# Low parts of the last even gates made by two transfers instead of a VectorE subtraction, with three-part even out-weights

## The chip, the cores and the metric

One core of a Trainium2 chip runs the whole program. The time is the device time of one execution in microseconds; the median of three runs is given. The profile is one more execution, with its own time.

## What is computed

```python
def _moe_ref(x, w_in, w_out):          # layer 1
    h = x @ w_in
    g = np.maximum(0.01 * h, h)
    return (g @ w_out).astype(np.float32)

def _moe2_ref(x, w_in, w_out):         # layer 2
    h = x @ w_in
    g = np.where(h > 0.0, h, np.exp(np.minimum(h, 0.0)) - 1.0)
    return (g @ w_out).astype(np.float32)
...
    f = lower_bound + (1.0 - lower_bound) * sigmoid(f_logit)
    h = f[:, t] * h + (1.0 - f[:, t]) * x[:, t]    # for t in range(6080), y[:, t] = h
...
    x = attn_out.reshape(6080, 256)    # then layer 1, then layer 2; w_in 256 x 2048, w_out 2048 x 256
```

A gated scan over 6080 rows of 256 values feeds two feed-forward layers. All data are 32-bit floats.

## The kernel before

**Tiles and stages.** The 6080 rows are cut into 12 chunks (eleven of 512 rows, the second of 448), counted here c0 to c11. Each layer's 2048 hidden columns are cut into four groups, q0 to q3. A step of the program is one (layer, chunk, group): the products of the chunk with the group's in-weights (`wI`), the activation, and the products of the gates with the group's out-weights, which add into the chunk's output banks. In a group the 128-column blocks with odd numbers and those with even numbers are kept apart: odd gates `aO` with weights `wO`, even gates `aE` with weights `wE`.

**Two parts for each operand.** TensorE multiplies in `float32r`. To keep more bits, every operand is split: the high part is a copy rounded to `float32r` (ScalarE, line 797 for gates), the low part is the value minus the high part (VectorE, line 801 for gates). A product is three matmuls, in `mm3` (lines 617 to 619): high by high, high weight by low gate, low weight by high gate. Gates lie in buffers of the pool `op`, 16 KB a partition, high part in the first half, low part in the second. There are seven of them.

**Fewer products.** The in-products of most steps, and the odd out-products of some, use a scheme of seven products where eight stand in the plain form (`seven` says where; lines 908 and 923 make the operands). The even gates always go the plain way, `straight("aE", "E", j)`.

**Order.** Nothing is issued while the kernel's Python runs through the steps. Each operation is given to `Plan` with a cost, a lateness (`late`), what it waits for, and what it takes from or gives back to a pool. `Plan.emit` then walks through a clock of its own and fixes the order of instructions on each engine. So the lateness written for an operation decides how many other matmuls are put ahead of those that need it.

**Around the change.** In layer 1 the even gates of a step are a Prelu (line 723) of `h`; in layer 2 they are made on VectorE in line 745 after a minimum (lines 738 or 740) and an exponential (line 743). Both rest on line 668, which adds the last in-product of the step. SP issues all transfers: the loads of x and f (line 560), layer 1's output to DRAM and back (989, 605), the weights of layer 2, which are split while layer 1 runs, put into DRAM (399, 401) and brought back over those of layer 1 between the layers (414), and the results (1002). GpSimd (POOL) does one operation on each weight as it is loaded (line 368) and otherwise nothing.

Of the kernel before, what the change touches and what calls it, by code (L numbers as in the profile page):

```python
# [9 lines left out]
F32 = mybir.dt.float32  # L10
# [102 lines left out]
def kernel(  # L113
# [54 lines left out]
    SEVEN = {1: (1, 2), 2: (0, 1)}  # L168

    def sums(l, u):  # L170

        return u[0] == "I" or u[0] == "O" and u[1] in SEVEN[l]

    def stored(u):
# [4 lines left out]
    size = {u: SO if u[0] == "E" or u[0] == "O" and not any(u[1] in v for v in SEVEN.values()) else SI for u in units}  # L179
    w = {u: const.tile([P, 2 * size[u]], F32R, name=f"w{u[0]}{u[1]}") for u in units}  # L180
    w2d = {u: dram.tile([P, 2 * stored(u)], F32, name=f"w2d{u[0]}{u[1]}") for u in units}
# [15 lines left out]
        "op": tiles(7, [P, 4 * CH], F32R, "op"),  # L197
# [22 lines left out]
    DMA, LATE, FAR, SGN = 0.475, 2.3, 4.5, 0.8  # L220

# [31 lines left out]
    def seven(l, c, q):  # L253

        return q in SEVEN[l] and not (l == 1 and c < 3) and not (l == 2 and c == NC - 1)

# [55 lines left out]
    def weights(l, u, due, gate=()):  # L312
# [41 lines left out]
        def lo():  # L354

            return w[u][:, size[u] : size[u] + m] if l == 1 else src()
# [29 lines left out]
        def src():  # L386
            return val()[:, :m]

        m = stored(u) if l == 2 else SO
        cp = act(s1(m), None, lambda: nc.scalar.copy(out=hi(), in_=src()), made,  # L390
                 take=[(b, "sp", "ws")] if l == 2 else [])
        sb = dve(v1(m), due, lambda: nc.vector.tensor_tensor(
            out=lo(), in0=src(), in1=hi().bitcast(F32), op=ALU.subtract,
        ), [cp], give=[(b, "wf", "ws")] if l == 1 else [])
        if l == 1:
            (wplain if aside else wdone)[l, u] = [sb]
            return
        was2.append(cp)
        a = dma(m / 586.0, None, lambda: nc.sync.dma_start(
            out=w2d[u][:, :m], in_=tile_("sp")[:, :m]), [cp], late=FAR)  # L400
        z = dma(m / 586.0, due, lambda: nc.sync.dma_start(
            out=w2d[u][:, m : 2 * m], in_=val()[:, :m]), [sb, a], give=[(b, "wf", "ws")], late=FAR)
# [3 lines left out]
    def reload(u, after):  # L406

        q = u[1] // 2 if u[0] == "I" else u[1]
        m = stored(u)

        def load(to, at, n):
            def run():
                dst, src = (t.rearrange("p (j m) -> p j m", j=2) for t in (w[u].bitcast(F32), w2d[u]))
# [5 lines left out]
        parts = [(0, 0, m // P)] if m < 8 * P else [(0, 7, 1), (1, 1, 6)]  # L419
        ready = wdone[2, u] + after  # L420
        wdone[2, u] = [dma(2 * part[2] * P / 590.0, due, load(*part), ready, late=LATE) for part in parts]

        def back(after):

            wdone[2, u] = [dma(0.5, due_in[-1 - NQ] - 3.0, load(0, 0, 1), after, late=LATE)]

        return back

    def wop(u, s):

        return tuple(w[u][:, j * size[u] + s * P : j * size[u] + (s + 1) * P] for j in (0, 1))
# [50 lines left out]
    def rows(c, filled, take, read=()):  # L482

        n = sizes[c]
        xb = {"rows": {}}
        bt = take

        def part(j, k):
            return xb["p"][2][:, 4 * HC * j + k * n : 4 * HC * j + (k + 1) * n]

        last = []
        for k in range(KD):
            def word(k=k):
                return bt["bt"][2][:, k * n : (k + 1) * n]
# [105 lines left out]
    def fetched(c, gates, hold):  # L600
        n = sizes[c]
        bt = {"pool": "bt"}
        filled = []
        for k in range(KD):
            filled.append(dma(DMA, None, lambda k=k: nc.sync.dma_start(
                out=bt["bt"][2][:, k * n : (k + 1) * n], in_=y1d[c][k * P : (k + 1) * P, :],
            ), gates + yd[c] + filled[:1], take=[(bt, "bt", "bt")] if k == 0 else [], late=LATE))
        ys[c] = operands(c, filled, bt, (), hold)


    def mm3(ps, wop, a, start, stop, whole=False):


        n = ps.shape[-1]
        parts = [slice(0, n)] if n < CH or whole else [slice(0, HC), slice(HC, CH)]
        for z, s in enumerate(parts):
            nc.tensor.matmul(ps[:, s], wop[0], a[0][:, s], start=start and z == 0, stop=False, skip_group_check=True)  # L617
            nc.tensor.matmul(ps[:, s], wop[0], a[1][:, s], start=False, stop=False, skip_group_check=True)  # L618
            nc.tensor.matmul(ps[:, s], wop[1], a[0][:, s], start=False, stop=stop, skip_group_check=True)  # L619
# [6 lines left out]
    def group(i):  # L626
# [10 lines left out]
        if l == 1 and c < 3:  # L637
            wo["O"] = wplain.get((l, ("O", q))) or wo["O"]
# [114 lines left out]
        def pieces():  # L753
# [5 lines left out]
            for r, s, bank, done, home in (("O", 1, "Y", C11, "seed"), ("E", 0, None, C22, None),  # L759
# [10 lines left out]
                else:  # L770
# [8 lines left out]
                hi = act(s1(2 * h), None, lambda a=a, g=g, s=s: nc.scalar.copy(out=view(a, 0, s), in_=half(g, s)),  # L779
# [3 lines left out]
                gates[r, s] = dve(v1(2 * h), None, lambda a=a, g=g, s=s: nc.vector.tensor_tensor(  # L783
                    out=view(a, 1, s), in0=half(g, s), in1=view(a, 0, s).bitcast(F32), op=ALU.subtract), [hi])
                kept.setdefault(r, [first_, hi])

# [7 lines left out]
        for name, g, done in (("aO", gO, odd), ("aE", gE, even)):  # L794
            if name == "aO" and apart or final:
                continue
            hi = act(s1(2 * n), None, lambda name=name, g=g: nc.scalar.copy(out=gate(name, 0), in_=whole(g)),  # L797
# [4 lines left out]
                out=gate(name, 1), in0=whole(g), in1=gate(name, 0).bitcast(F32), op=ALU.subtract,  # L802
# [24 lines left out]
        def turned(r, s, part):  # L827
# [7 lines left out]
            def wide(z, j):  # L835
                return w[r, q][:, z * size[r, q] + j * D : z * size[r, q] + (j + 1) * D]

            def run(fresh):
                for j in (0, 1):
                    for t in tiles_:  # L840
                        dst = yb[s][2][:, t % 2 * D : (t % 2 + 1) * D]
                        for z in (0, 1):
                            nc.tensor.matmul(dst, ops(part, j, t), wide(z, j), start=s in fresh and t % 2 + j + z == 0,  # L843
                                             stop=False, skip_group_check=True)
                            if part:
                                break
# [181 lines left out]
    for i, (l, c, q) in enumerate(stream):  # L1028
        back = [firsts[i - 6] if i >= 6 else None]
        if q == 0:  # L1030
            hold = firsts[i - 1 : i - 1 + 1] if i > 4 else []
# [13 lines left out]
        if l == 2 and c == NC - 1 and q in SEVEN[2]:  # L1045
            backs["O", q]([last_use[q][1]])
        at = len(prods)
        o = group(i)
        if l == 1 and c in (1, 2):
            for z in ([q - 1] if q else []) + ([q] if q == NQ - 1 else []):  # L1050
                for u in (("I", 2 * z), ("I", 2 * z + 1)) if c == 1 else (("O", z),):
                    if sums(1, u):
                        finish(u, [prods[-1], outs[-1]])
        firsts.append(prods[at])
        if l == 1 or c == NC - 2:
            last_use[q] = (prods[-1], o)
# [31 lines left out]
```

## Time and profile before

| | |
|---|---|
| median of the three runs | 994.54 us (994.28 to 1003.21) |
| profiled execution, its own time | 995.75 us |
| span of the profile | 993.9 us |
| TensorE matmuls busy | 982.4 us, 99% of the span, 8234 instructions |
| VectorE | 878.9 us, 88%, 1356 |
| ScalarE | 774.5 us, 78%, 1139 |
| GpSimd | 37.8 us, 4%, 38 |
| transfers on SP's queue | 73.08 MB, 27.4% of 16 DMA engines |

The profiled execution's time is 1.85 us longer than its span, and 1.2 us longer than the median. Busy times of matmuls overlap (each is 0.28 us long and the next starts 0.11 us later), so the distance from one start to the next is what a matmul costs. L with a number is a line of the kernel; `op<-ws,op` reads: writes a buffer of `op`, reads one of `ws` and one of `op`.

### The profile page before, as it was taken

What the parts mean: (1) busy time and instruction counts of PE and PEld (TensorE: products, weight loads), DVE (VectorE), ACT (ScalarE), POOL (GpSimd) and SP (SyncE); (2) the same over time, 40 slices, a digit from 0 to 9 for tenths busy, and PEclk for the clock granted to TensorE, in tenths of its full rate; (3) what the DMA queues carried; (4) which work ended last, traced back from release to release, by engine and by line L of the source; (5) the groups of instructions that cost most, each with busy time, mean ns of one, the idle gap of its engine ahead of it and who ended that gap; (6) DMA issues with size and microseconds to landing.
All of it is one profiled execution on the core that took longest, in us unless ns stands there. A gap on an engine that the chain in (4) does not pass through costs nothing.

```text
span 993.9 us, 20119 instructions
## 1 busy us (share of the span) xinstructions
PE 982.4 (99%) x8234; PEld 969.8 (98%) x8234; DVE 878.9 (88%) x1356; ACT 774.5 (78%) x1139; POOL 37.8 (4%) x38
## 2 busy tenths in 40 slices
PE   7999999999999999999999999999999999999998
PEld 6999999999999999999999999999999999999998
DVE  7899989999999999886678888988988989889875
ACT  6777787887878878867687878788877888788864
POOL 1122000100000010100000000000000000000000
PEclk9999999999999999999999999999999999999999
DMA  6542304435254443302760101101111021010110
GB/s 185 138 115 56 82 12 115 119 97 155 80 150 142 108 138 112 85 23 95 260 226 22 22 22 41 22 23 22 31 35 22 23 44 22 22 23 22 32 22 22
DMA packets 159853, 74.36 MB, mean 75 GB/s; under 512 B 133520, under 2 KB 147600, under 8 KB 159760
## 3 DMA queue, kind: packets, MB, share of 16 engines
q1 hardware_dynamic: 159760, 73.08, 27.4%
q8 instruction: 64, 1.05, 0.4%
q14 instruction: 29, 0.24, 0.1%
HBM read 48.01 MB, written 25.03 MB: 73 GB/s over the span
## 4 chain that ended last, share of the span: by engine, by line
PE 94%; DVE 4%; POOL 1%; issue 1%; DMA 0%; ACT 0%; DVEq 0%; SPq 0%
PE bank L617 28%; PE bank L618 28%; PE bank L619 28%; PE bank L843 2%; PE seed L619 2%; PE seed L618 2%; PE seed L617 2%; POOL ws L368 1%; DVE ws L378 0%; DVE op L801 0%; DVE ws L374 0%; DVE h L279 0%; DVE bt L585 0%; DMA raw<-in_f_logit_dram 0%; DVE up L365 0%
## 5 line engine op out<-in xcount | busy, mean ns | idle before, releaser
L617 PE MATMUL bank<-op,wI 128*128 128x256 f32 (+2 forms) x1136 | 318.1, 280 | 0.8 <-ACT sn L665 0.6
L618 PE MATMUL bank<-op,wI 128*128 128x256 f32 (+2 forms) x1136 | 317.3, 279 | 1.4 <-DVE op L498 1.4
L619 PE MATMUL bank<-op,wI 128*128 128x256 f32 (+2 forms) x1136 | 316.9, 279 | 0.0
L617 PEld LDWEIGHTS bank<-op,wI 128*128 128x128 f32 x1136 | 213.6, 188 | 3.7 <-ACT sn L665 0.9
L618 PEld LDWEIGHTS bank<-op,wI 128*128 128x128 f32 x1136 | 213.5, 188 | 3.6 <-DVE op L498 2.1
L619 PEld LDWEIGHTS bank<-op,wI 128*128 128x128 f32 x1136 | 213.5, 188 | 0.4
L618 PE MATMUL bank<-op,wE 128*128 128x256 f32 (+2 forms) x662 | 190.9, 288 | 0.0
L617 PE MATMUL bank<-op,wE 128*128 128x256 f32 (+2 forms) x662 | 190.8, 288 | 0.0
L619 PE MATMUL bank<-op,wE 128*128 128x256 f32 (+2 forms) x662 | 190.7, 288 | 0.0
L618 PE MATMUL bank<-op,wO 128*128 128x256 f32 (+2 forms) x672 | 187.7, 279 | 0.0
L617 PE MATMUL bank<-op,wO 128*128 128x256 f32 (+2 forms) x672 | 187.7, 279 | 0.0
L619 PE MATMUL bank<-op,wO 128*128 128x256 f32 (+2 forms) x672 | 187.6, 279 | 0.0
L668 DVE TENSOR_TENSOR h<-bank,sn 128x512 f32<-128x512 f32 (+1 forms) x176 | 120.1, 682 | 36.3 <-PE bank L619 30.0
L617 PEld LDWEIGHTS bank<-op,wO 128*128 128x128 f32 x672 | 126.3, 188 | 0.4
L619 PEld LDWEIGHTS bank<-op,wE 128*128 128x128 f32 x662 | 124.3, 188 | 2.3
L619 PEld LDWEIGHTS bank<-op,wO 128*128 128x128 f32 x672 | 126.2, 188 | 0.3
L618 PEld LDWEIGHTS bank<-op,wO 128*128 128x128 f32 x672 | 126.2, 188 | 0.3
L665 ACT COPY sn<-bank 128x512 f32<-128x512 f32 (+1 forms) x176 | 102.6, 583 | 30.0 <-PE bank L619 28.3
L617 PEld LDWEIGHTS bank<-op,wE 128*128 128x128 f32 x662 | 124.5, 188 | 1.3
L618 PEld LDWEIGHTS bank<-op,wE 128*128 128x128 f32 x662 | 124.3, 188 | 1.2
L801 DVE TENSOR_TENSOR op<-h,op 128x1024 fp32r<-128x1024 f32 (+1 forms) x78 | 95.6, 1226 | 8.9 <-ACT op L797 8.4
L801 DVE TENSOR_TENSOR op<-ws,op 128x1024 fp32r<-128x1024 f32 (+1 forms) x72 | 86.1, 1209 | 15.1 <-ACT op L797 15.1
(112 smaller groups left out, 1770.5 us busy)
## 6 DMA issues: line engine op xcount, KB each, us to landing
ws<-in_moe_w_in_dram SPq DMA_DIRECT2D x32, 255.6 KB, 3.7
ws<-in_moe_w_out_dram SPq DMA_DIRECT2D x32, 255.6 KB, 3.3
w2dI<-ws SPq DMA_DIRECT2D x16, 448.0 KB, 3.0
wI<-w2dI SPq DMA_DIRECT2D x8, 896.0 KB, 5.8
y1d<-t SPq DMA_DIRECT2D x22, 256.0 KB, 2.0
bt<-y1d SPq DMA_DIRECT2D x22, 256.0 KB, 2.8
raw<-in_f_logit_dram SPq DMA_DIRECT2D x80, 64.0 KB, 3.0
raw<-in_x_dram SPq DMA_DIRECT2D x80, 64.0 KB, 2.5
```

The lines of the kernel that those rows point to most:

```text
L368: sg = pool(SGN, None, lambda: nc.gpsimd.tensor_scalar(out=fr(), in0=top().bitcast(I8), scalar1=2.0, scalar2=-2.0, op0=ALU.min, op1=ALU.ma ...
L617: nc.tensor.matmul(ps[:, s], wop[0], a[0][:, s], start=start and z == 0, stop=False, skip_group_check=True)
L618: nc.tensor.matmul(ps[:, s], wop[0], a[1][:, s], start=False, stop=False, skip_group_check=True)
L619: nc.tensor.matmul(ps[:, s], wop[1], a[0][:, s], start=False, stop=stop, skip_group_check=True)
L665: return act(s1(2 * h), None, lambda: nc.scalar.copy(out=ps(name), in_=ps("X")), after, take=[(b, name, "sn")])
L668: return dve(v1(2 * h), None, lambda: nc.vector.tensor_tensor(out=half(name, s), in0=two(ps(bank)), in1=two(ps(sn)), op=ALU.add), after, **k)
L801: gates[name] = dve(v1(2 * n), None, lambda name=name, g=g: nc.vector.tensor_tensor(out=gate(name, 1), in0=whole(g), in1=gate(name, 0).bit ...
L843: nc.tensor.matmul(dst, ops(part, j, t), wide(z, j), start=s in fresh and t % 2 + j + z == 0, stop=False, skip_group_check=True)
```

## The change

Three things are edited, and the set of products stays as it is (the table `SEVEN` is written in another form with the same members; `back`, `finish` and the names `parts`, `cut`, `pieces` follow from that).

1. For q3 of both layers (`LOWS`), except the very last step, the even gates' low part is no longer a VectorE subtraction. A transfer on SP copies the gates into the low half of the `op` buffer, ScalarE writes minus the high part into the high half, and a transfer issued by GpSimd adds the high half onto the low half (`late_low`). The planner is told 0.475 + 3.0 us for the copy and 1.3 + 5.0 us for the addition.
2. For this the high part of all even gates is stored negated, so the even weights are kept in three parts: high, minus high, and minus low. `mm3` and `turned` take the second for the product with the gates' high part. The weight tiles `wE` grow from 2 to 3 parts, ScalarE makes the new one, and layer 2's `wE` goes to DRAM and back with it.
3. The pool `op` has six buffers in place of seven.

```diff
-    w = {u: const.tile([P, 2 * size[u]], F32R, name=f"w{u[0]}{u[1]}") for u in units}
-    w2d = {u: dram.tile([P, 2 * stored(u)], F32, name=f"w2d{u[0]}{u[1]}") for u in units}
+    def parts(u):
+        return 3 if u[0] == "E" else 2
+    w = {u: const.tile([P, parts(u) * size[u]], F32R, name=f"w{u[0]}{u[1]}") for u in units}
+    w2d = {u: dram.tile([P, parts(u) * stored(u)], F32, name=f"w2d{u[0]}{u[1]}") for u in units}
...
-        "op": tiles(7, [P, 4 * CH], F32R, "op"),
+        "op": tiles(6, [P, 4 * CH], F32R, "op"),
...
+    LOWS = ((1, NQ - 1), (2, NQ - 1))
+    SWD, CCE, COPY = 1.3, 5.0, 3.0
...
+        ends = [sb]
+        if minus:
+            turned = w[u][:, m : 2 * m] if l == 1 else None
+            ends.append(act(s1(m), due, lambda: nc.scalar.mul(
+                out=turned if l == 1 else tile_("sp").bitcast(F32R)[:, m : 2 * m], in_=hi().bitcast(F32), mul=-1.0), [cp]))
...
+        three = ((0, 0), (0, 1), (1, 0)) if len(wop) == 2 else ((1, 0), (0, 1), (2, 0))
...
+            for t, (g, v) in enumerate(three):
+                nc.tensor.matmul(ps[:, s], wop[g], a[v][:, s], start=start and z == t == 0, stop=stop and t == 2,
+                                 skip_group_check=True)
...
+        def late_low(g, done):
+
+            def low():
+                return gate("aE", 1).bitcast(F32)
+
+            got = plan.add("-", 0.0, None, lambda: None, done, take=[(b, "aE", "op")])
+            cp = dma(DMA, None, lambda: nc.sync.dma_start(out=low(), in_=whole(g)), [got], late=COPY)
+            hi = act(s1(2 * n), None, lambda: nc.scalar.mul(out=gate("aE", 0), in_=whole(g), mul=-1.0),
+                     [got, *highs[-1:]])
+            free([cp, hi], [(b, g, home)])
+            ad = pool(SWD, None, lambda: nc.gpsimd.dma_start(
+                out=low(), in_=gate("aE", 0).bitcast(F32), accum_op=ALU.add), [hi, cp], late=CCE)
+            highs.append(hi)
+            for s in (0, 1):
+                tops["E", s], gates["E", s] = hi, ad
+            gates["aE"] = ad
...
+            if name == "aE" and (l, q) in LOWS:
+                late_low(g, done)
+                continue
```

In layer 2, TensorE's order ahead of the even products of q3 of chunk c4, before (lines 617 to 619 are the three matmuls of `mm3`; `wO3`, `wE3` are q3's out-weights, `wI2` and `wI3` in-weights of the next chunk's q0):

```order
L619 MATMUL bank1_116<-op0_122,wO3_77 128x256
L617 MATMUL bank4_119<-op4_126,wI2_65 128x256
L618 MATMUL bank4_119<-op4_126,wI2_65 128x256
L619 MATMUL bank4_119<-op4_126,wI2_65 128x256
L617 MATMUL bank4_119<-op4_126,wI3_66 128x256
L618 MATMUL bank4_119<-op4_126,wI3_66 128x256
L619 MATMUL bank4_119<-op4_126,wI3_66 128x256
L617 MATMUL bank2_117<-op3_125,wE3_78 128x256
```

The same place of the changed kernel (the three matmuls now share line 632; DMASW is the semaphore of a transfer issued by GpSimd):

```order
L632 MATMUL bank3_118<-op0_122,wO3_77 128x256 x6
L632 MATMUL bank6_121<-op4_126,wI2_65 128x256 x3
L632 MATMUL bank6_121<-op4_126,wI3_66 128x256 x3
L632 MATMUL bank2_117<-op4_126,wI2_65 128x256 [waits Activation_49]
...
L632 MATMUL seed0_114<-op1_123,wI3_66 128x256 x3
L632 MATMUL bank2_117<-op4_126,wI2_65 128x256 [waits Activation_49]
L632 MATMUL bank2_117<-op4_126,wI2_65 128x256 x2
L632 MATMUL bank2_117<-op4_126,wI3_66 128x256 x3
L632 MATMUL bank4_119<-op3_125,wE3_78 128x256
L632 MATMUL bank4_119<-op3_125,wE3_78 128x256 [waits DMASW2_49]
```

Three more pairs of in-products now stand between the odd and the even products: from the last in-matmul of the step itself to the first even one there are 115 matmuls before and 127 after, and the second even one is the first that waits for the added low part.

VectorE's order around q3's even gates of layer 2, before (line 745 makes the gates, the second line 801 their low part):

```order
L668 TENSOR_TENSOR h0_130<-bank5_120,sn2_139 128x2x256 [waits PE_49]
L740 TENSOR_SCALAR ws2_136<-h0_130 128x1024 [waits DVE_49]
...
L745 SCALAR_TENSOR_TENSOR ws2_136<-ws2_136,h0_130 128x1024 [waits Activation_49]
L971 TENSOR_TENSOR h1_131<-h1_131 128x256
L801 TENSOR_TENSOR op4_126<-ws0_134,op4_126 128x1024 [waits Activation_49]
L801 TENSOR_TENSOR op0_122<-ws2_136,op0_122 128x1024 [waits Activation_49]
```

The same place of the changed kernel (lines 682, 754, 759 and 838 are the former 668, 740, 745 and 801):

```order
L682 TENSOR_TENSOR h2_131<-bank2_117,sn2_138 128x2x256 [waits PE_49]
L748 SCALAR_TENSOR_TENSOR ws1_134<-ws1_134,seed0_114 128x2x256 [waits Activation_49]
L754 TENSOR_SCALAR ws2_135<-h2_131 128x1024 [waits DVE_49]
L748 SCALAR_TENSOR_TENSOR ws1_134<-ws1_134,bank3_118 128x2x256
L1017 TENSOR_TENSOR raw2_141<-h0_129 128x512
L759 SCALAR_TENSOR_TENSOR ws2_135<-ws2_135,h2_131 128x1024 [waits Activation_49]
L838 TENSOR_TENSOR op4_126<-ws1_134,op4_126 128x1024 [waits Activation_49]
```

The even gates' subtraction is gone from VectorE; the odd gates' one stays, and 23 instructions of 1358 leave the engine in all.

SP's order around the same gates in the changed kernel (line 618 loads the next chunk's input, line 1043 stores results; the copy of line 809 is new):

```order
L618 DMA bt0_128<-y1d5_100 128x512 [waits DMAHW4_49,DVE_49]
L618 DMA bt0_128<-y1d5_100 128x512 [waits DMAHW5_49]
L809 DMA op4_126<-ws1_134 128x1024 [waits DMAHW6_49,DVE_49,PE_49]
L1043 DMA out_0_dram<-t1_143 32x16x32 [waits DMAHW7_49,DVE_49]
...
L1043 DMA out_0_dram<-t0_142 32x16x32 [waits DMAHW2_49,DVE_49]
```

The copy stands between the loads and the stores, so SP comes to the stores behind it only when the gates are done. On GpSimd the additions alternate in layer 1 with the operations on weights (line 375, the former 368); in layer 2 they stand alone. 23 copies and 23 additions are new, 12 in layer 1 and 11 in layer 2.

## Rows read from the trace of the kernel before

**Rows 1.** Waits of TensorE: who waited for whom, total us, times, longest us.

```profile
PE bank L547 <- DMA raw<-in_f_logit_dram: 1.7, 2, 0.9
...
PE bank L618 <- DVE op L498: 1.4, 3, 0.6
PE bank L617 <- ACT sn L665: 0.6, 1, 0.6
PE seed L619 <- DVE wI L392: 0.3, 1, 0.3
```

**Rows 2.** Windows of 20 us, busy us (instructions) by engine, TensorE's granted clock, DMA share.

```profile
20.00:40.00 20.00, 19.01 (x127) 17.42 (x126) 18.20 (x26) 15.11 (x27) 4.23 (x5) 1.00 0.45 126
...
820.00:840.00 20.00, 20.00 (x177) 20.00 (x176) 19.26 (x31) 15.79 (x23) 0.00 (x0) 1.00 0.03 4
```

**Rows 3.** Groups by shape, TensorE's weight loads for the even products.

```profile
L617 PEld LDWEIGHTS bank<-op,wE 128*128 128x128 f32 x662 | 124.5, 188 | 1.3
...
L618 PEld LDWEIGHTS bank<-op,wE 128*128 128x128 f32 x662 | 124.3, 188 | 1.2
```

**Rows 4.** Groups by shape, the gates' split (busy us, mean ns) and the minimum of line 740.

```profile
L801 DVE TENSOR_TENSOR op<-h,op 128x1024 fp32r<-128x1024 f32 x70 | 86.7, 1239 | 7.2 <-ACT op L797 6.8
L801 DVE TENSOR_TENSOR op<-ws,op 128x1024 fp32r<-128x1024 f32 x66 | 79.5, 1220 | 14.7 <-ACT op L797 14.7
...
L797 ACT CAST op<-ws 128x1024 fp32r<-128x1024 f32 x66 | 68.1, 1050 | 2.9 <-DVE ws L734 1.4 <-DVE ws L745 1.3
...
L740 DVE TENSOR_SCALAR ws<-h 128x1024 f32<-128x1024 f32 x23 | 15.9, 690 | 0.4
```

**Rows 5.** Timeline of ScalarE near the start: start us, us, what.

```profile
26.98 0.57 ACT L496 CAST op<-bt 128x448 fp32r<-128x448 f32 x1 [0.30 <-DVE bt L585]
```

**Rows 6.** Timeline of VectorE near the start, the low part that follows.

```profile
28.21 0.61 DVE L498 TENSOR_TENSOR op<-bt,op 128x448 fp32r<-128x448 f32 x1
```

**Rows 7.** Timeline of TensorE, layer 2, q3: last in-matmul and first even matmul.

```profile
776.57 0.28 PE L619 MATMUL bank<-op,wI 128*128 128x256 f32 x1
...
789.60 0.28 PE L617 MATMUL bank<-op,wE 128*128 128x256 f32 x1
```

**Rows 8.** Timeline of VectorE, the even gates of the same step.

```profile
779.92 1.22 DVE L745 SCALAR_TENSOR_TENSOR ws<-ws,h 128x1024 f32<-128x1024 f32 x1
```

**Rows 9.** Timeline of SP, 770 to 782 us.

```profile
776.07 0.82 SPq L605 DMA_DIRECT2D bt<-y1d  x2
```

**Rows 10.** Timeline of TensorE, layer 1, q3: last in-matmul and first even matmul.

```profile
254.91 0.28 PE L619 MATMUL bank<-op,wI 128*128 128x256 f32 x1
...
267.26 0.28 PE L617 MATMUL bank<-op,wE 128*128 128x256 f32 x1
```

**Rows 11.** Timeline of ScalarE, the even gates of that step.

```profile
256.38 1.06 ACT L723 ACTIVATE h<-h 128x1024 f32<-128x1024 f32 x1
```

**Rows 12.** DMA issues: count, KB each, median us from issue to landing.

```profile
w2dO<-ws SPq DMA_DIRECT2D x4, 512.0 KB, 3.5
...
wE<-w2dE SPq DMA_DIRECT2D x4, 512.0 KB, 4.5
wO<-w2dO SPq DMA_DIRECT2D x2, 768.0 KB, 5.3
...
wI<-w2dI SPq DMA_DIRECT2D x8, 896.0 KB, 5.8
```

**Rows 13.** GpSimd's operations on tile ws: duration ns min/median/max, first and last start.

```profile
L368 POOL TENSOR_SCALAR ws<-ws x32: 636/812/4309, 7.9 to 397.7; 128x512 f32<-128x512 int8 x32
```

**Rows 14.** Line 399's stores of 256 to 512 KB during layer 1.

```profile
DMA to landing us min/median/max: 2.0/2.7/4.4
```

**Rows 15.** Windows of the stretches after q3's even gates (columns as in rows 2).

```profile
257.70:267.70 10.00, 10.00 (x90) 10.00 (x90) 9.90 (x15) 9.93 (x17) 0.87 (x1) 1.00 0.60 172
...
499.70:509.70 10.00, 10.00 (x91) 10.00 (x90) 5.93 (x10) 7.24 (x11) 0.00 (x0) 1.00 0.73 286
...
781.40:791.10 9.70, 9.70 (x88) 9.70 (x88) 8.97 (x18) 7.13 (x10) 0.00 (x0) 1.00 0.01 3
```

More of the change, by code (lines that the diff above doesn't have):

```diff
@@ L167 @@
     SI, SO = 7 * P, 2 * D
-    SEVEN = {1: (1, 2), 2: (0, 1)}
+    SEVEN = {(1, 1): range(3, 12), (1, 2): range(3, 12), (2, 0): range(0, 11), (2, 1): range(0, 11)}
     def sums(l, u):
-        return u[0] == "I" or u[0] == "O" and u[1] in SEVEN[l]
+        return u[0] == "I" or u[0] == "O" and len(SEVEN.get((l, u[1]), ())) > 0
     def stored(u):
@@ L253, in seven @@
     def seven(l, c, q):
-        return q in SEVEN[l] and not (l == 1 and c < 3) and not (l == 2 and c == NC - 1)
+        return c in SEVEN.get((l, q), ())
     due_in = [0.0]
@@ L354, in lo @@
         def lo():
-            return w[u][:, size[u] : size[u] + m] if l == 1 else src()
+            at = (parts(u) - 1) * size[u]
+            return w[u][:, at : at + m] if l == 1 else src()
         def val():
@@ L418, in reload, with back @@
         due = due_in[first[2, "w", q]] + (-12.0 if u[0] == "I" else 0.0)
-        parts = [(0, 0, m // P)] if m < 8 * P else [(0, 7, 1), (1, 1, 6)]
+        pieces = [(0, 0, m // P)] if m < 8 * P else [(0, 7, 1), (1, 1, 6)]
         ready = wdone[2, u] + after
-        wdone[2, u] = [dma(2 * part[2] * P / 590.0, due, load(*part), ready, late=LATE) for part in parts]
-        def back(after):
-            wdone[2, u] = [dma(0.5, due_in[-1 - NQ] - 3.0, load(0, 0, 1), after, late=LATE)]
+        wdone[2, u] = [dma(parts(u) * piece[2] * P / 590.0, due, load(*piece), ready, late=LATE) for piece in pieces]
+        def back(i, after):
+            wdone[2, u] = [dma(0.5, due_in[i] - 3.0, load(0, 0, 1), after, late=LATE)]
         return back
     def wop(u, s):
-        return tuple(w[u][:, j * size[u] + s * P : j * size[u] + (s + 1) * P] for j in (0, 1))
+        return tuple(w[u][:, j * size[u] + s * P : j * size[u] + (s + 1) * P] for j in range(parts(u)))
     S4, A11, A22, A12, S1, S2, S3 = range(7)
@@ L835, in wide @@
             def wide(z, j):
-                return w[r, q][:, z * size[r, q] + j * D : z * size[r, q] + (j + 1) * D]
+                at = z * size[r, q] + j * D
+                return w[r, q][:, at : at + D]
+            three = ((0, 0), (0, 1), (1, 0)) if r == "O" else ((0, 1), (0, 2), (1, 0))
             def run(fresh):
@@ L841, in run @@
                         dst = yb[s][2][:, t % 2 * D : (t % 2 + 1) * D]
[L842 to L846, printed above, removed]
+                        for y, z in three:
+                            if y == part:
+                                nc.tensor.matmul(dst, ops(part, j, t), wide(z, j),
+                                                 start=s in fresh and t % 2 + j + part == 0 and z == three[0][1],
+                                                 stop=False, skip_group_check=True)
             out_((2 - part) * len(tiles_), run, (s,), [(gates if part else tops)[r, s], *wo[r]])
@@ L1030 @@
         if q == 0:
[L1031 removed]
+            hold = firsts[-1:] if i > 4 else []
             if l == 1:
```

55 lines of the change are left out of this document (28 added, 27 removed).

## The prediction

> **What bounds the kernel now.** I read the waits of TensorE first, since a kernel whose matmuls are 99% busy can only gain what TensorE still waits. The view names 7 waits with some 7 us in all, and over half of that lies in the first five microseconds, before there is data [rows 1]. What is left is one wait of three times for VectorE's line 498 near the start and three single ones, some 2.5 us in all. Then the windows: from 40 us on each 20 us stretch holds nearly 20 us of matmul at a granted clock of 1.00, which is 2.4 GHz, while VectorE stands at 19.26 of 20 in layer 2 [rows 2]. The reader is to see that a busy VectorE delays nobody here. The third thing to read is the distance between two starts: from the last in-matmul of a step to its first even matmul 13.03 us pass for 115 matmuls, 0.1133 us each [rows 7]. The changed kernel issues the same 8224 matmuls of the same widths, so TensorE's stream keeps its length, and the change can only alter the waits in it.
>
> **What is removed.** 23 subtractions leave VectorE, 11 of full width in layer 1 and 10 in layer 2 at 1.24 and 1.22 us, and two narrower ones: 28 us of busy time [rows 4]. On the path lies only what TensorE waited for VectorE, 1.7 us of it, most of it at the start where no subtraction has left yet. I take a gain of 0.5 us, with 0 and 2.5 us (all the waits that are left) as ends.
>
> **What is added at no cost.** ScalarE makes the negated part of `wE` eight times, some 0.6 us each (the time of its 512-column casts, [rows 5] shows 0.57 for 448 columns), and multiplies by -1 where it copied; it has a fifth of its time free [rows 2]. The one place near the path is the first: the new operation stands ahead of the cast of line 496, which ran from 26.98 to 27.55 [rows 5]. It would end some 0.3 us later, and VectorE takes up the low part only at 28.21 [rows 6], so it stays covered; uncovered it would cost 0.6 us once. The even products change their order of weights, and no two neighbours share a weight any more. The trace shows that this was worth nothing: the second of two equal loads takes 188 ns like the first [rows 3]. The layer-2 `wE` is stored with 256 KB more and comes back as 768 KB, 5.3 us in place of 4.5 [rows 12]: 3.2 us more of transfers in a stage whose DMA engines are 73% busy [rows 15]. No wait of TensorE for a weight's return stands in the view of waits, so I take 0, with 3.2 us as the other end.
>
> **The new path, and its room.** In the 23 steps the low part now comes from copy, GpSimd's issue and addition, one after the other. The room for it is read from the trace and the order. In layer 2 the last in-matmul starts at 776.57 [rows 7] and the gates are done at 779.92 + 1.22 = 781.14 [rows 8], 4.57 us later. In the changed order the first matmul that waits is the 128th after it: 128 x 0.1133 = 14.50 us. The room is 14.50 - 4.57 = 9.93 us, and that order stands for nine of the eleven steps of layer 2; the two beside the narrow chunk have 0.2 and 0.6 us less. VectorE's order between the last in-product and line 745 (now 759) holds one operation more, line 1017, but the minimum comes one operation earlier, so I leave the 4.57 us as they are. In layer 1 the gates are done at 256.38 + 1.06 = 257.44 [rows 11], 2.53 us after the last in-matmul [rows 10]; the order has 115 matmuls there in five steps, 121 in two, 109 in two and 127 in one, which leaves 10.6, 11.3, 9.9 and 12.0 us. The first two chunks have 10.7 us or more by the same count.
>
> The trace of before has no copy inside SBUF and no adding transfer. For the copy of 512 KB the nearest rows are a store of 512 KB, 3.5 us, and a load of 512 KB, 4.5 us [rows 12]; I take 3.5, since it reads the same memory and the stage of the 4.5 was crowded. For GpSimd's issue the nearest row is its operation on weights, 0.64 to 4.31 us with a median of 0.81 [rows 13]; I take 0.85. For the addition the ends are 3.5 (as a plain 512 KB) and 6.6 us, where 896 KB take 5.8 and a line through 512 and 896 KB gives 6.6 for twice 512 KB [rows 12]; I take 4.7, near the middle. The sum is 3.5 + 0.85 + 4.7 = 9.05 us, under the room of 9.93 by 0.9, so layer 2 costs nothing. The ends are 3.5 + 0.64 + 3.5 = 7.6 and 4.5 + 0.85 + 6.6 = 12.0 us, the latter 2.0 us late in each step.
>
> The addition reads two streams of 512 KB where a copy reads one; the trace of before can't show what that costs. The Trainium skill says in "Collectives: The Full Stack", section "The bandwidth ceiling: the fold count and why AG ≠ RS ≠ AR", that an adding transfer is slow not for its arithmetic but because it needs two source reads on the same read ring, and halves the rate. That speaks against this change: by it the addition would be nearer to the 6.6 us, the sum 10.95 us, and each step of layer 2 late by 1.0 us.
>
> **Queues.** On SP the copy waits for the gates. Ahead of it stand the next chunk's two input loads, which were issued at 776.07, five microseconds before the gates [rows 9], and behind it only stores of results, whose buffers VectorE's transposes need again a chunk later. In layer 1 loads of x and f and of weights stand behind it, which wait for buffers of their own. GpSimd's additions alternate in layer 1 with its weight operations; it is idle nearly all the time, and a weight operation delayed by an addition feeds a layer that is hundreds of microseconds away.
>
> **Other traffic.** In layer 2 the DMA engines are free in that stretch, 1% [rows 15]. In layer 1 they are 18 to 60% busy there, the fullest at 257.7 [rows 15], and stores that take 2.7 us in the middle took up to 4.4 there [rows 14]. With 1.7 us more the 9.05 would become 10.75, a little late against 10.6 and 0.8 us late against 9.9. I count 1.5 us for some five full steps together, with 0 and 12 us as ends (1.7 us for copy and addition both, in six steps, less the 1.5 us spare). Layer 1's last addition meets the return of the layer-2 weights [rows 15]: I take 0.6 us once, with 0 and 4 as ends.
>
> **The sum.** -0.5 + 0 + 0 + 1.5 + 0.6 = +1.6 us on the profiled execution's 995.75, which gives 997.35, and on the median, 1.2 us lower, 994.54 + 1.6 = 996.1 us.
>
> **Rivals.**
> *The path is longer than its room (slower).* The point from which it decides is 9.9 us for copy, issue and addition. At 10.95 us layer 2 loses 1.0 x 11, layer 1 0.35 x 5 + 1.05 x 2, some 15 us: 1010 us. At 12.0 it is 2.1 x 11 + 1.4 x 5 + 0.7 x 2 + 2.1 x 2 = 36 us: 1031 us. For it speaks the addition's double reading, against it that DMA is nearly idle in layer 2 and that 9.05 rests on rows of the same size. Chance 0.18.
> *GpSimd's issue is stretched by VectorE (slower).* Its operation on weights took up to 4.31 us while VectorE was full [rows 13, 2]. Were each issue 3 us longer, the sum would be 12 us and the time again 1031. It would need this in most steps, while the median of the 32 is 0.81. Chance 0.05. The Trainium skill, "SBUF — State Buffer", section "Who interferes with whom", narrows this: only VectorE's two-port forms hold up the writing of descriptors. The row that shows such a form is line 740, 690 ns for 1024 columns where line 801 takes 1220 [rows 4]; by that rule an issue is delayed by at most 0.7 us, which the 0.9 us of room still hold.
> *Six `op` buffers are too few.* In the changed order 54 of ScalarE's 304 writes into `op` wait for TensorE, 19 before. If each of the 35 new waits made an operand 0.3 us late (the small waits of TensorE are 0.3 to 0.6 us, [rows 1]), it would be +10 us: 1005 to 1007 us. Against it: the releasing matmul stands well ahead of the reader of the buffer in TensorE's own order. Chance 0.07, half of it over 1%.
> *VectorE's relief pays (faster).* The bound is the 2.5 us of waits, 992.0 us; more than 1% would need TensorE's stream to be shorter. Chance of over 1%: 0.02.
>
> **How the numbers follow.** A measurement of this kernel tells about 1%, 10 us, from no change. The forecast, hidden but for a few steps (-2.5 to +10 us), has 0.68. Faster is 0.02. Of the rivals' 0.30 that are slow, 0.07 stay within 1%. So same is 0.75 and slower 0.23. The range begins at 992.0, where all waits are gone, and ends at 1012, past the nearer price of the first rival; above it lie the second's 0.05 and half of the first's, some 0.15, below it 0.02.
>
> **What would show it.** Matmul counts and VectorE less by 28 us show the removal. The waits of TensorE should hold no line with more than some 3 us for GpSimd's transfer, above all none in layer 2; the DMA issues should show the copy near 3.5 us and the addition near 4.7. A wait of q3's even matmuls of 1 us or more in each chunk is the first rival; long issues on POOL are the second; waits for other `op` writers on ScalarE and VectorE the third. The forecast is wrong if the addition is slower than 5.6 us.

## The result, and the profile after

The changed kernel took 1004.77 us (median of 13 runs, 999.82 to 1006.87) against 995.46 us (13 runs, 994.28 to 1003.78) for the kernel before. The ratio on record is 1.0065, 95% interval 1.0042 to 1.0088; it is not that of the two medians, which is 1.0094. That is slower, by less than the 1% that the prediction called the bound, and inside its range; the forecast of 996.1 us was 8.7 us too low. The runs of each kernel here fall into bunches several us apart, by slow spacings of matmuls that the experiments show, so a median also tells in which bunch most runs were. The profiled execution of the changed kernel took 1004.97 us.

First the page: busy us, share of the span and instructions of each engine.

```profile
PE 988.8 (99%) x8234; PEld 973.3 (97%) x8234; DVE 858.7 (86%) x1333; ACT 780.7 (78%) x1147; POOL 55.9 (6%) x61
```

TensorE has the same 8234 matmuls, VectorE 23 instructions less. The two full-width groups of VectorE's split, which answer to [rows 4], have lost 25.2 us (141.0 in place of 166.2), with the mean of one as before. All durations of VectorE add up to 26.7 us less; its busy time on the page fell by 20.2 us, since there overlaps count once. The groups now:

```profile
L838 DVE TENSOR_TENSOR op<-h,op 128x1024 fp32r<-128x1024 f32 x59 | 72.6, 1230 | 10.6 <-ACT op L833 10.4
L838 DVE TENSOR_TENSOR op<-ws,op 128x1024 fp32r<-128x1024 f32 x56 | 68.4, 1222 | 12.1 <-ACT op L833 11.2
```

The new path stands in the DMA issues (count, KB each, median us to landing) and in the queues (packets, MB, share of 16 engines); these answer to [rows 12]:

```profile
q0 software_dynamic: 3312, 11.93, 6.3%
...
op<-op POOLq DMA_DIRECT2D x21, 512.0 KB, 4.7
...
op<-h SPq DMA_DIRECT2D x11, 512.0 KB, 3.2
...
op<-ws SPq DMA_DIRECT2D x10, 512.0 KB, 2.9
```

Both count from the start of the issue. The addition's 4.7 us thus hold GpSimd's issue too, where the sum had 0.85 + 4.7; the copy takes 2.9 to 3.2 in place of 3.5. But a median hides a tail. The same additions, asked for by the tile that they write (GpSimd's issue in ns min/median/max; who waited, us, times; landing min/median/max):

```profile
L813 POOL DMA_DIRECT2D op<-op x23: 859/862/1021, 89.8 to 956.2; - x23
...
  PEld bank L632: 3.9, 5
  PE bank L632: 2.7, 3
...
DMA to landing us min/median/max: 4.2/4.7/10.1
```

By this view five steps of 23 waited, and one addition took 10.1 us. The waits of TensorE, which answer to [rows 1], name three of them and a snapshot (line 679) that cost 0.6 us before:

```profile
PE bank L632 <- DMA op<-op: 2.7, 3, 1.3
...
PE bank L632 <- ACT sn L679: 0.9, 2, 0.5
PE bank L632 <- DVE op L511: 0.8, 2, 0.6
```

These lines explain less than 3 of the 10.2 us by which the last matmul starts later in the new trace. (The span is 9.3 us longer: from the last start to the end 3.9 us pass in place of 4.8.) For the rest I took the start of every matmul in each trace and sorted the distance to the next. A spacing that is over 25 ns above the usual (113.3 ns at 256 columns, 226 at 512, 198 at 448, 100 at 224, 57 at 128) is a gap, and what is above the usual is its length. The other spacings at 256 columns are nearly all of two kinds: 112 to 115 ns, and 116 to 120 ns, at a granted clock of 1.00 both; from 116 ns on the excess over 113.3 is summed apart, as slow spacings. All kernels of this study, in us:

```
               gaps by stretch of the span            slow spacings  last
               0-40  40-200  200-560  560-end   all   number    us   start    rest
before         13.6     1.5      0.8      0.4  16.2      739   3.5   989.1   969.4
after          14.6     0.8      5.9      3.3  24.6     1130   5.3   999.3   969.4
again          13.6     0.8      9.1      3.3  26.7     1246   5.8  1002.0   969.4
ops6           14.2     1.4      0.2      0.4  16.2     1629   7.5   993.0   969.3
no_low         13.3     0.9      0.1      0.4  14.7      463   2.4   986.4   969.4
no_low_again   13.9     0.8      0.0      0.4  15.1     3280  14.8   999.2   969.3
cover          13.6     1.0      0.3      0.4  15.3     2488  11.3   996.0   969.4
low_l1         13.5     0.8      4.2      0.4  18.9      890   4.2   992.5   969.4
low_l2         14.2     0.9      0.0      3.3  18.4     3474  15.7  1003.5   969.4
late_dve       13.7     0.8      0.8      5.1  20.3     2558  11.6  1001.3   969.4
split          14.1     2.1      9.2      2.0  27.4     1517   7.0  1003.8   969.4
tight          13.3     1.0     11.5      1.3  27.1     2576  11.7  1008.1   969.4
quiet          13.4     0.8      1.3      0.4  15.9      687   3.3   988.5   969.4
busy           13.3     1.0      6.3      0.4  21.0      786   3.7   994.1   969.4
```

What is left when gaps and slow spacings are taken off is 969.3 or 969.4 us in every trace, so the account is complete. The change added 8.4 us of gaps (5.1 in layer 1 from 200 us on, 2.9 behind 560 us, 1.0 among the first loads, less 0.7 from 40 to 200) and 1.8 us of slow spacings: 10.2 us. The 1.0 us is not the change's: the run again, of the same kernel, has 13.6 us there like before.

The two new kinds of gap, one of each. In layer 1 the last group's even products start, one matmul runs, and the next waits for the addition that GpSimd issued at 262.48 (timeline of TensorE: start, us, what, idle before it):

```profile
268.04 1.52 PE L632 MATMUL bank<-op,wI 128*128 128x256 f32 x12
269.40 0.28 PE L632 MATMUL bank<-op,wE 128*128 128x256 f32 x1
270.94 1.33 PE L632 MATMUL bank<-op,wE 128*128 128x256 f32 x9 [1.27 <-DMA op<-op]
```

By the starts the five waits for additions (at 228.4, 269.4, 352.7, 394.3 and 518.0 us) cost 0.4, 1.5, 0.3, 0.9 and 1.1 us, 4.3 us before rounding, of which 0.11 us each is a second gap, one matmul later.

In layer 2 a single product waits for an addition, 0.09 us at 922.3 us (it starts 0.04 us after the landing, as the five do). What every chunk there has is another gap: the products on bank X, its snapshot and the next product on X follow each other with too little between them (TensorE, then ScalarE):

```profile
676.35 1.52 PE L632 MATMUL bank<-op,wI 128*128 128x256 f32 x12
677.72 0.84 PE L632 MATMUL seed<-op,wI 128*128 128x256 f32 x6
678.55 0.96 PE L632 MATMUL bank<-op,wI 128*128 128x256 f32 x6
679.36 1.86 PE L632 MATMUL bank<-op,wE 128*128 128x256 f32 x15
```

```profile
677.00 0.82 ACT L961 CAST op<-ws 128x768 fp32r<-128x768 f32 x1
677.91 0.59 ACT L679 COPY sn<-bank 128x512 f32<-128x512 f32 x1
```

Six matmuls take 0.68 us, so the products of 678.55 would have started at 678.40; the snapshot ran until 678.50. They start 0.15 us late, and the next start is 0.81 us behind them in place of 0.68. In the kernel before, at the same chunk, twelve even products of the last group stood behind the first products on X (they start at 670.17) and six more behind the products on `seed`:

```profile
670.06 0.28 PE L619 MATMUL bank<-op,wI 128*128 128x256 f32 x1
670.17 0.28 PE L617 MATMUL bank<-op,wE 128*128 128x256 f32 x1
...
671.53 0.28 PE L617 MATMUL seed<-op,wI 128*128 128x256 f32 x1
...
672.22 0.28 PE L617 MATMUL bank<-op,wE 128*128 128x256 f32 x1
```

```profile
670.37 0.59 ACT L665 COPY sn<-bank 128x512 f32<-128x512 f32 x1
```

The snapshot ended at 670.96, and the next products on X start behind the last of the six, at 672.9. Now all of these even products start at 679.36, behind this place, and nothing covers it. That is 0.24 to 0.29 us in ten chunks and 0.6 us in the last.

### The profile page after: what moved, and what is told of

Its sections match the earlier page's. It is cut to its first block, busy times and chain, and to the rows that moved or that the text cites. A ratio compares the mean times of both kernels' runs of the same rounds, so it can differ in the third digit from the quotient of the medians.

```text
span 1003.2 us, 20318 instructions
## 1 busy us (share of the span) xinstructions
PE 988.8 (99%) x8234; PEld 973.3 (97%) x8234; DVE 858.7 (86%) x1333; ACT 780.7 (78%) x1147; POOL 55.9 (6%) x61
## 4 chain that ended last, share of the span: by engine, by line
PE 91%; DMA 5%; DVE 2%; ACT 1%; issue 1%; DVEq 0%; SPq 0%; POOLq 0%; ACTq 0%
PE bank L632 82%; PE seed L632 6%; DMA op<-op 4%; PE bank L885 2%; DMA raw<-in_x_dram 1%; PE bank L560 0%; DVE op L838 0%; DMA op<-h 0%; DMA raw<-in_f_logit_dram 0%; DVE wE L400 0%; ACT h L737 0%; ACT op L833 0%; DVE ws L381 0%; ACT h L705 0%; ACT t L583 0%
## 5 line engine op out<-in xcount | busy, mean ns | idle before, releaser
L632 PE MATMUL bank<-op,wI 128*128 128x256 f32 (+2 forms) x3408 | 471.2, 280 | 1.9 <-ACT sn L679 0.9
L632 PEld LDWEIGHTS bank<-op,wI 128*128 128x128 f32 x3408 | 429.5, 188 | 9.4 <-ACT sn L679 3.0
L632 PE MATMUL bank<-op,wE 128*128 128x256 f32 (+2 forms) x1986 | 290.9, 289 | 2.9 <-DMA op<-op 2.7
L632 PE MATMUL bank<-op,wO 128*128 128x256 f32 (+2 forms) x2016 | 272.9, 280 | 0.0
L632 PEld LDWEIGHTS bank<-op,wE 128*128 128x128 f32 x1986 | 255.6, 188 | 8.9 <-DMA op<-op 3.9
L632 PEld LDWEIGHTS bank<-op,wO 128*128 128x128 f32 x2016 | 250.3, 188 | 1.0
L632 PE MATMUL seed<-op,wI 128*128 128x256 f32 (+1 forms) x576 | 80.7, 277 | 0.0
L964 DVE TENSOR_TENSOR op<-h,op 128x1024 fp32r<-128x1024 f32 (+2 forms) x58 | 66.7, 1150 | 7.8 <-ACT op L961 7.4
L632 PEld LDWEIGHTS seed<-op,wI 128*128 128x128 f32 x576 | 72.8, 188 | 0.1
L833 ACT ACTIVATE op<-h 128x1024 fp32r<-128x1024 f32 (+1 forms) x66 | 69.2, 1049 | 2.0 <-PE bank L632 1.1
```

The lines of the kernel that those rows point to most:

```text
L632: nc.tensor.matmul(ps[:, s], wop[g], a[v][:, s], start=start and z == t == 0, stop=stop and t == 2, skip_group_check=True)
L833: hi = act(s1(2 * n), None, lambda name=name, g=g: nc.scalar.mul(out=gate(name, 0), in_=whole(g), mul=-1.0 if name == "aE" else 1.0), done ...
L964: lows.append(dve(v1((e - s) * h), None, lambda s=s, e=e, src=src: nc.vector.tensor_tensor(out=part(1, s, e), in0=src(), in1=part(0, s, e) ...
```

## The experiments

Every kernel was timed in 5 rounds beside the kernel before. Two theories stood at the start: the additions come late under other traffic (layer 1), and the later place of the last group's even products leaves a snapshot uncovered (layer 2). Rivals: six `op` buffers, the third part of the weights, transfers that cost by being there, and chance.

**ops6.** The kernel before with

```diff
-        "op": tiles(7, [P, 4 * CH], F32R, "op"),
+        "op": tiles(6, [P, 4 * CH], F32R, "op"),
```

> The kernel before, with six op buffers in place of seven and nothing else. If six buffers are what costs (operands made late), most of the 9.3 us between the two kernels is here: 1000 to 1005 us. If the transfers and the places of the last group's matmuls cost it, the time stays within 1.5 us of before, 994 to 997.

998.44 us, ratio 1.0024 (1.0011 to 1.0037), between the two ranges that were expected. The gaps are those of before, 16.2 us; its trace is longer by slow spacings alone, 7.5 us in place of 3.5. So the buffers (8 KB a partition each, not the 16 KB named ahead of the prediction) make no operand late. Why five of its seven runs took over 998 us, where one of 19 of before in the same rounds did, is not shown.

**no_low, low_l1, low_l2.** The changed kernel with

```diff
-    LOWS = ((1, NQ - 1), (2, NQ - 1))
+    LOWS = ()                # no_low;  ((1, NQ - 1),) low_l1;  ((2, NQ - 1),) low_l2
```

> The changed kernel with no step in the list for transfers: VectorE makes every low part, the even weights stay in three parts and the op buffers stay six. If the transfers and what they move in TensorE's order cost the time, 995 to 998 us (what is left is the start, 1.7 us by 40 us of the trace). If the third part of the weights or the six buffers cost it, over 1000 us.

> Transfers in layer 1 alone (twelve steps). If the three waits for the last addition in layer 1 (2.7, 3.0 and 1.3 us) and the stretches behind them are the cost, nearly all of it is here: 1001 to 1004 us. If the cost is the uncovered snapshot of each layer-2 chunk, 997 to 999.

> Transfers in layer 2 alone (eleven steps). If the late additions of layer 1 are the cost, 996 to 999 us: the start and 0.25 us a chunk. If the snapshot that is uncovered in each layer-2 chunk and the slow matmuls behind it are the cost, 1000 to 1004.

no_low 994.35 us, a little below what was expected, ratio 1.0010 (0.9981 to 1.0040); low_l1 1000.12, 1.0055 (1.0037 to 1.0073); low_l2 1003.57, 1.0094 (1.0071 to 1.0118). The gaps part cleanly: with transfers in layer 1 alone 4.2 us stand in layer 1 and 0.4 behind it, with transfers in layer 2 alone 0.0 and 3.3. So both theories hold for the gaps, and the weights in three parts add none. (The expectation of low_l1 misreads the view of the waits: three waits of 2.7 us in total, the longest 1.3.) The time of low_l1 lies between the two ranges that were expected. The time of low_l2 fits neither expectation by its mechanism: its trace (of a run of 1009.34 us) has the 3.3 us of gaps and 15.7 us of slow spacings, most of them in one stretch from 195 to 555 us, where it holds no transfer of this kind at all.

**late_dve.** no_low with the place of the products, without the transfers:

```diff
+            if name == "aE" and q == NQ - 1:
+                gates[name] = plan.add("-", 0.0, None, lambda: None, [gates[name]], late=8.4)
```

> VectorE makes every low part, as in the run without transfers, but the planner is told that the even low part of the last group lands 8.4 us after VectorE ends, so the last group's even products stand where the changed kernel has them: 18 matmuls later in each full chunk of layer 2, 6 to 18 later in layer 1. If their place is what costs layer 2 its 2.9 us (a product that waits for the snapshot of bank X, with nothing between), that stays here: small gaps of 0.2 us in each layer-2 chunk, 2 to 3 us in all, 995 to 998 us, and no wait for a transfer in layer 1. If the transfers themselves make those gaps, there are none: 993 to 995.

1003.97 us, ratio 1.0055 (1.0031 to 1.0080). Layer 1 has 0.8 us of gaps. Layer 2 has 5.1, more than the 2 to 3 that were expected: 4.1 at the same place of its chunks, and 1.0 in one wait for VectorE at 754.3 us:

```profile
676.65 1.52 PE L632 MATMUL bank<-op,wI 128*128 128x256 f32 x12
678.01 0.84 PE L632 MATMUL seed<-op,wI 128*128 128x256 f32 x6
678.99 0.95 PE L632 MATMUL bank<-op,wI 128*128 128x256 f32 x6
```

The start at 678.99 is 0.30 us late, without any transfer: the place makes the gap. (TensorE's order as a whole is not that of the changed kernel, but around this place it is.) The time is above what was expected, by 11.6 us of slow spacings.

**split and tight.** Every transfer kept, another lateness told to the planner. (The expectation of split misstates two of its numbers: layer 1 was told 3.0 and 8.0 us.)

```diff
-    SWD, CCE, COPY = 1.3, 5.0, 3.0
+    SWD, CCE, COPY = 0.9, {1: 8.0, 2: 4.2}, {1: 3.0, 2: 3.0}     # split, indexed by layer
+    SWD, CCE, COPY = 0.9, 3.9, 2.6                               # tight
```

> The changed kernel with every transfer kept, and the planner told another lateness for each layer: the copy 4.0 and the addition 9.0 us in layer 1 (3.0 and 4.2 in layer 2), so that the last group's even products stand 12 to 24 matmuls later than without transfers in layer 1 and 6 later in layer 2. If the lateness in layer 1 and the uncovered snapshot in layer 2 are the cost, the gaps of layer 1 fall from 5.9 us to below 2 and those of layer 2 from 2.1 to below 1: 995 to 999 us. If the transfers cost by being there, it stays at 1001 to 1005.

> The changed kernel with the planner told 2.6 us for the copy and 3.9 for the addition, which puts the last group's even products back where they stand without transfers, in both layers. By the lateness theory the small gaps of layer 2 go (2 us less) and the layer-1 waits grow, by 0.7 us in each of six crowded chunks: 1003 to 1009 us. If lateness isn't it, 1000 to 1003.

tight: 1013.70 us, ratio 1.0156 (1.0106 to 1.0205). With the products back in their old place the gaps of layer 2 fall to 1.3 us (1.0 of it by two late additions) and those of layer 1 double to 11.5, with this line in the waits:

```profile
PE bank L632 <- DMA op<-op: 7.8, 6, 2.6
```

Its slow spacings, 11.7 us, put it above the range that was expected. split: 1010.18 us, ratio 1.0118 (1.0075 to 1.0162), and here my expectation fell. The waits for additions shrank as meant, but the gaps of layer 1 grew from 5.9 to 9.2 us, and those of layer 2 fell to 2.0 and not below 1, since one addition there came 1.2 us late (at 560.6 us):

```profile
PE bank L632 <- ACT sn L679: 4.2, 7, 1.0
...
PE bank L632 <- DMA op<-op: 1.4, 2, 0.9
```

Further back, the even products uncover the snapshots of layer 1 too: earlier they wait for the addition, later the in-products wait for the snapshot. Between the two there was no place in the crowded chunks that cost nothing, among the three that were tried.

**quiet and busy.** Transfers in half of layer 1, by what else the queues moved:

```diff
-            if name == "aE" and (l, q) in LOWS:
+            if name == "aE" and (l, q) in LOWS and l == 1 and c in (0, 1, 2, 3, 9, 10):   # quiet
+            if name == "aE" and (l, q) in LOWS and l == 1 and c in (4, 5, 6, 7, 8, 11):   # busy
```

> Transfers in layer 1 alone, and there only in the six chunks where the trace of the changed kernel shows other queues at 42 GB/s or less beside the addition (chunks 0 to 3, 9 and 10); VectorE makes the rest. If the other traffic is what makes the additions late, each lands 4.2 to 4.8 us after its issue starts, no product of the last group waits for one, and the gaps between 200 and 560 us stay under 1 us: 993 to 997 us. If the transfers or their places cost by themselves, half of the loss of the run with all twelve is here: 997 to 999.

> The other half of layer 1: transfers only in the six chunks where other queues moved 130 to 246 GB/s beside the addition (chunks 4 to 8 and 11). If traffic makes them late, additions of 5.3 to 10 us, three to five waits for them and 3 to 6 us of gaps between 200 and 560 us, as in the changed kernel: 998 to 1002 us. Otherwise 996 to 998.

quiet: 995.19 us, ratio 0.9977 (0.9952 to 1.0002), landing

```profile
DMA to landing us min/median/max: 4.5/4.6/5.0
```

and no wait for one; 1.3 us of gaps in layer 1, 0.3 more than the bound that was expected. busy: 1000.76 us, ratio 1.0032 (1.0007 to 1.0058), 6.3 us of gaps in layer 1, of which 4.4 in four waits for additions, landing

```profile
DMA to landing us min/median/max: 6.4/7.1/10.5
```

Six transfers each, and only those beside other traffic cost anything. No run took the traffic out of a crowded chunk; that it is the traffic rests on the landings of the two groups and on the windows. The windows of the changed kernel, from an issue to the end of its packets, show the same in one trace (last two columns: share of the DMA engines, GB/s, the addition's own included):

```profile
262.48:270.57 8.09, 7.20 (x64) 7.00 (x62) 6.44 (x10) 8.05 (x14) 1.71 (x2) 1.00 0.93 232
...
428.23:432.93 4.70, 4.70 (x44) 4.70 (x43) 4.54 (x9) 4.04 (x8) 0.88 (x1) 1.00 0.72 133
508.94:518.73 9.79, 8.78 (x75) 8.38 (x73) 7.94 (x14) 8.30 (x13) 0.86 (x1) 1.00 1.00 298
632.26:636.47 4.21, 4.21 (x40) 4.21 (x39) 3.03 (x7) 3.78 (x5) 0.86 (x1) 1.00 0.66 125
```

**again, no_low_again, cover.** The changed kernel and no_low a second time, unaltered, and no_low with one number for the planner:

```diff
-            C22 = add("hE", 0, "R", "z4", [pR, z4], take=[(b, "hE", "h")], give=[(b, "z4", "sn")])
+            C22 = add("hE", 0, "R", "z4", [pR, z4], take=[(b, "hE", "h")], give=[(b, "z4", "sn")],
+                      late=0.2 if (l, c, q) == (1, 5, 1) else 0.0)
```

> The changed kernel once more, for a second trace of it. If its cost is in fixed places, the same gaps stand there: 2 to 6 us in layer 1 behind the last group's additions, 2 to 3 us in layer 2, and a time of 1000 to 1006 us. If it is chance, gaps and slow stretches stand elsewhere.

> The run without transfers once more, with a second trace: even weights in three parts, six op buffers, VectorE for every low part. If it is as fast as the kernel before or faster, 993 to 996 us with gaps under 1.5 us after 40 us of the span; runs above 999 us, if the trace is of one, by a long stretch of matmuls at 118 ns and not by gaps.

> The run without transfers, and the planner told that one addition of VectorE (the first even half of chunk 5's second group, in the wait that ends at 193.7 us) lands 0.2 us later, so that six products of other work stand ahead of the product that waited for it 60 ns. If that short gap is what starts the stretch of matmuls at 118 ns (194 to 554 us, 12.4 us in all) in half of that kernel's runs, then no gap is at 193 to 195 us here and at least ten of twelve runs are at 992 to 997 us: faster than the kernel before by 0.1 to 0.3%. If the stretch starts by chance whatever stands there, about half of the runs are again at 1004 to 1005.

again: 1005.48 us, ratio 1.0072 (1.0044 to 1.0100). Four of the five late additions of layer 1 stand at the same chunks and layer 2 has the same 3.3 us, so the loss is in fixed places. Layer 1 has 9.1 us of gaps, above the 2 to 6 that were expected, 3.0 of them by the clock (last section). no_low_again: 1004.62 us, ratio 1.0033 (1.0000 to 1.0065), from the kernel that had 994.35. Its trace has the gaps of no_low, 15.1 and 14.7 us, and 14.8 us of slow spacings in place of 2.4: from 194.5 to 554.1 us nearly every matmul of 256 columns starts 118 ns after the one before. One product of 12 in each, no_low first; it takes 1.36 us to the next start there and 1.41 here:

```profile
300.92 1.52 PE L632 MATMUL bank<-op,wO 128*128 128x256 f32 x12
302.28 0.84 PE L632 MATMUL bank<-op,wI 128*128 128x256 f32 x6
```

```profile
305.31 1.58 PE L632 MATMUL bank<-op,wO 128*128 128x256 f32 x12
306.72 0.87 PE L632 MATMUL bank<-op,wI 128*128 128x256 f32 x6
```

The same 50 us of the span hold 437 recorded matmuls in one and 421 in the other, at the same granted clock:

```profile
300.00:350.00 50.00, 50.00 (x437) 49.73 (x436) 49.78 (x82) 42.40 (x66) 6.68 (x4) 1.00 0.48 135
```

```profile
300.00:350.00 50.00, 50.00 (x421) 49.74 (x420) 48.46 (x81) 42.45 (x66) 3.53 (x3) 1.00 0.46 127
```

cover was meant to remove the gap ahead of that stretch, but 0.2 us was too little for the planner: its order is that of no_low on every engine. So it tests nothing of its expectation, and serves as a third trace of the same instructions: 1000.48 us, ratio 1.0018 (0.9984 to 1.0051), 15.3 us of gaps and 11.3 us of slow spacings, this time in several stretches, the longest from 376 to 550 us. Of the 36 runs of this one order 13 took 992 to 997 us and 23 took 998 to 1006. So the slow spacings differ from run to run of the same instructions, by up to 12 us.

## Why the prediction held, and where its sum was short

**The durations** held with something to spare: copy 2.9 to 3.2 us (3.5 said), issue and addition together 4.7 in the median (5.55 said), so some 7.8 us for the path in place of 9.05; VectorE's durations less by 26.7 us (28 said). TensorE's matmuls are the same in number, though 8234 and not 8224. In layer 2 the path fits its room: one wait of 0.1 us for an addition there, in low_l2 (at 763.7 us) as in the changed kernel. The rival of a stretched issue is refuted by the 859 to 1021 ns of all 23 issues, that of the six buffers by ops6, and the gain from VectorE's relief is not shown: TensorE's gaps from 40 to 200 us are 0.7 us shorter, but no_low, where VectorE makes every low part, has 0.9 us there too, in place of 1.5.

**The term that was mis-sized** is "other traffic": 1.5 us for five steps and 0.6 for the last addition of layer 1. The trace has 4.3 us for these five waits, the last addition's 1.1 among them; busy with six transfers has 6.3 us of gaps in layer 1 (0.8 before). The working said 1.7 us more for copy and addition both; in the six crowded chunks the packets of the additions alone ended 5.3 to 9.8 us after the issue began, where those of a free one end at 4.2. The text named an addition slower than 5.6 us as the sign of a wrong forecast; over all 23 it takes 3.8 us behind the issue in the median, in busy 6.2 (7.1 with 0.88 for the issue). The mechanism, and that it is layer 1 that pays, was right.

**The step that is missing** is what the even products covered. I asked whether their operand comes in time at the new place, not what their leaving uncovers at the old one: 2.9 us of gaps in layer 2, shown by late_dve without a transfer. A wait for the snapshot in the changed kernel's layer 1 (0.8 us at 516.4) is of the same kind.

**What no step could hold**: 1.8 us of slow spacings in this pair of traces, which by the three traces of one order can be 12 us. They do not explain the loss: without them, by an estimate from the table, the two profiled executions would take 992.3 and 999.7 us (995.75 - 3.5 and 1004.97 - 5.3), and no run of either kernel lies below. But they are not the same chance for every order either. Of the 8 us of low_l2 over before some 3 are gaps of layer 2 and the rest, in its one trace, is of this kind; all six of its runs took over 1001 us, where one of 19 of before in the same rounds did. Whether moving the products makes the slow spacings more frequent stays open.

That the result lies in the range is in part luck. The range had its room for the rival of the longer path, which did not come; what came were late additions at twice their term and 2.9 us that stood in no term.

**On the adding transfer**, the Trainium skill ("Collectives: The Full Stack", section "The bandwidth ceiling: the fold count and why AG ≠ RS ≠ AR") has an adding step at half the rate of a copy, because it needs two source reads on the same read ring. The packets agree: in the step at 632 us, where no other queue moved anything, the 512 KB of the addition passed from 1.43 to 4.20 us after the issue's start, 2.8 us, and those of the copy ahead of it from 1.13 to 2.56, 1.4 us. What does not double is the time ahead of the first packet, so the whole came to 4.7 us with the issue, and not to the 0.85 + 6.6 of my upper end.

## What to carry to other kernels

When a wait-tolerant block of work is moved back in TensorE's order, look at its old place too: it may be the cover of a hand-over between two other engines, and then neither place is free. A transfer that replaces an engine's operation should be costed with the traffic of each stage it runs in; six additions in quiet chunks were hidden, six in crowded ones came with some 5 us of gaps. In a kernel that is bound by TensorE at 99%, compare the starts of its matmuls between traces before believing a cause: gaps, spacings and the rest add up, and the waits view named about a third of the gaps that this change added.

## What the runs showed of the hardware

TensorE's matmuls of 256 columns have two spacings at a granted clock of 1.00, 113.3 and 117.8 ns. In the 14 traces there are 37 stretches of over 12 us in which most spacings are slow (ten or more of any 15 neighbours). 35 of them begin within 2 us of a gap (over 25 ns, as above), and a small one was enough, 35 ns at 293.4 us in cover. The same gap need not do the same: 60 ns at 193.7 us in no_low_again began some 360 us of slow spacings, 73 ns at the same product in no_low 6 us. 22 of the 37 end at a group of six products of 512 columns, and so did those 6 us, and eight at the next gap; but the stretch of 360 us passed nine such groups. What sets and ends the slow spacing stays open: that a gap causes it was not tested, since cover did not move what it was meant to move.

Behind the first 40 us, every gap of more than 0.12 us in these traces is followed by a second one of about 0.11 us, one matmul later, but for the two where the clock fell. A long wait can cost the clock: in again the last addition of layer 1 kept TensorE waiting 2.2 us from 515.95, and the granted clock was 0.50 (1.2 GHz) afterwards, so that one matmul started 0.38 us behind the one before and 27 more 213 ns apart, a loss of 3.0 us; the windows (TensorE's busy time and count behind the sum of the stretch, granted clock third from the end):

```profile
516.00:518.00 2.00, 0.22 (x2) 0.03 (x1) 2.00 (x3) 1.96 (x4) 0.00 (x0) 0.87 0.93 275
518.00:524.00 6.00, 5.83 (x27) 5.83 (x28) 1.31 (x3) 0.00 (x0) 0.00 (x0) 0.50 0.07 26
524.00:530.00 6.00, 6.00 (x52) 6.00 (x52) 5.61 (x11) 5.34 (x8) 0.00 (x0) 0.98 0.90 322
```

The waits of the trace of after, up to 1.5 us, left the clock at 1.00, and so did one of 2.0 us in busy (to 517.2 us) and one of 2.4 us in tight (to 395.1 us); one of 2.7 us in tight (to 519.8 us) was followed by 0.50. So a wait of 2.2 us lost the clock and one of 2.4 us kept it: the length alone did not decide.
